# Chunk attention and a Mish feed-forward by seven products: results of a set summed and passed through Mish in place in PSUM, lower parts moved back, weight sums from slot 14, more lower parts on GpSimd

## The chip, the core and the metric

The kernel runs on one core of a Trainium2 chip. Its engines each work through their own instructions in order: TensorE (PE in the profile; PEld is its weight loads), VectorE (DVE), ScalarE (ACT), GpSimd (POOL) and SyncE (SP), which issues nearly all DMAs. An instruction waits on semaphores for what it needs, and everything behind it on its engine waits with it. The metric is the device time in microseconds (us). The kernel before was timed in three runs with a median of 862.57 us, from 860.93 to 862.65.

## What is computed

Attention runs inside chunks of 64 tokens, then a feed-forward layer with the Mish activation follows over 4608 tokens with model width 512 and inner width 2048.

```python
scores = scale * np.matmul(q_c, k_c.transpose(0, 1, 2, 4, 3))     # chunks of 64
attn = softmax(scores)
x = np.matmul(attn, v_c)                                          # (4608, 512) after reordering
h = x @ w_in                                                      # (4608, 2048)
g = h * np.tanh(np.log1p(np.exp(h)))                              # Mish
out = g @ w_out                                                   # (4608, 512)
```

All is float32. The large products are made of three products of rounded parts: each factor is split into a higher part (a cast) and a lower part (the value less its higher part), and high by high, high by low and low by high are added up in PSUM. So each factor costs a cast, called "hi", and a subtraction, called "lo".

## The kernel before, in words

**Two phases.** The first 1024 tokens go through a plain phase of 32 slots, `slot(s)`, s from 0 to 31 (`N` = 32). Slot s runs on TensorE the up projection of step s+1 (`up`), some attention, and the down projection of step s-1 (`down`). Beside it VectorE and ScalarE split the weights (done by slot 14), take Mish, cast (`g_hi`, L327 and L329) and subtract (`g_lo`, L334). The other 3584 tokens go through 32 sets, `s_set(z)`, z from 0 to 31, in four blocks of eight sets: a block is 896 tokens, a set is 256 columns of the inner width.

**A set** makes a 2 by 2 block product with seven products u0 to u6 instead of eight. The order of a set is written out by hand in `ORDER`, fourteen steps m = 0 to 13: the even steps are u0 to u6 (`s_up`, L675, six matmuls of 448 columns each), the odd ones are down projections (`s_down`, L697, six matmuls of 512 columns each) of the set before, d0 to d5, and at step 1 the last one, e6, of the set before that. At each step the program issues the matmuls, then attention that is planned for this step on TensorE, then for a down projection its sum (`s_out`, L724: VectorE adds the PSUM bank to the running sum), and then whatever `when(z, m, ...)` has put there, in the order in which it was put. (z, m) below is step m of set z.

The four results c11, c12, c22 and c21 of a set come out like this. u1 and u0 make c11, u2 and u4 with the copy "u2" make c12, and so on: u0, u3, u5 and u6 add up in one PSUM bank called al (two of them, in turn), u1 goes to a bank b, and u2 and u4 add up in a bank g. ScalarE copies three of these (`s_copy`, L739: "p1" at step 0, "p5" at step 4, "u2" at step 6) to SBUF. VectorE then adds (`s_c`, L748): c11 = b + p1 at step 2, c12 = g + u2 at step 8, c22 = al + p5 at step 10. c21 is al itself after u6. ScalarE takes Mish (`s_hi`, L760) and casts (L761), and VectorE subtracts (`s_lo`, L764): lo 11 at step 3, lo 12 at step 9, lo 22 at step 11, lo 21 at step 13. In the kernel before each c lies in SBUF, in a tile of the tag z.

Waits that tie TensorE to these: u4 adds onto g, so it waits for the copy p5; u5 adds onto al and waits for the copy u2; u6 adds onto al and waits for c22. In set 0 the banks b and g are the two halves of one PSUM tile, bg, and u2 waits for c11.

**The inputs of a block**, seven sums and views of x (`x_sum`, L624; k = 2, 5, 3, 4), are split in the last set of the block before (z = 7, 15, 23): ScalarE casts (`x_hi`, L629), and lo (`x_lo`, L633) runs on GpSimd for k in `LOW_BY_POOL` and on VectorE otherwise. For the first block this is done in slots 29 to 31 and in set 0, all on VectorE but the sum of k = 4. x_sum 4 reads what x_sum 3 wrote, x_hi 4 reads x_sum 4, x_lo 4 reads x_hi 4.

**Weights of the seven products** are made once, in slots 16 to 31: every second slot `t_sum` and `t_diff` (GpSimd, L479 and L493), one slot later `t_hi` (ScalarE, L499), and one slot after that `t_lo` (VectorE, L505) and four DMAs to DRAM (L510). `tset, part = divmod(s - NF, 2)` with NF = 16 says which. They share the four buffers of the tag st with the tiles of `store`, which copies a finished output block out of PSUM at slot 16 and in set 0 (L361 on VectorE, L363 on ScalarE, L367 the DMAs), and with the sum x_sum 2.

**Attention in the sets** (`plan_pair`) starts at the steps `STARTS`; a pair has its maximum on VectorE one and four steps after the start, its subtraction at two and five, Exp on ScalarE (with a table load) at six.

Of the kernel before, what the change touches and what calls it, by code (L numbers as in the profile page):

```python
# [9 lines left out]
F32 = mybir.dt.float32  # L10
# [4 lines left out]
AF = mybir.ActivationFunctionType  # L15
# [3 lines left out]
P = 128  # L19
# [6 lines left out]
def kernel(  # L26
# [437 lines left out]
    def keep_weights(f):  # L464

        s, e = divmod(f, 2)
        for k, half in ((0, 0), (1, 1)) if e == 0 else ((4, 1),):
            src = w_part(f, slice(0, 2))[:, :, half * 2 * P : (half + 1) * 2 * P]
            nc.sync.dma_start(out=raw(dwi_of(s, k)), in_=raw(src))
        nc.sync.dma_start(out=raw(dwo[s][:, e]), in_=raw(w_part(f, slice(2, 4))))  # L470
# [30 lines left out]
    def t_lo(s):  # L501
        d = tw.pop(s)
        for i in range(2):
            o = d["s", i]
            nc.vector.tensor_tensor(  # L505
                out=o[:, :, 1], in0=d["t"][:, 2 * i : 2 * i + 2], in1=raw(o[:, :, 0]), op=ALU.subtract
            )
            for e in range(2):
                k = (2, 3, 5, 6)[2 * i + e]
                nc.sync.dma_start(out=raw(dwi_of(s, k)), in_=raw(o[:, e]))  # L510
# [89 lines left out]
            ps = d["p", t].rearrange("p g c k -> p (g c) k").unsqueeze(1)  # L600
            small_mm(o[:, :, t : t + 1], d["v"][:, t : t + 1], ps, FIRST)

    LOW_BY_POOL = (2, 5, 6)
    xo = {}
    xs = {}

# [24 lines left out]
    def x_lo(b, k):  # L631
        engine = nc.gpsimd if b and k in LOW_BY_POOL else nc.vector
        engine.tensor_tensor(  # L633
            out=xo[k][:, 1], in0=x_src(b, k), in1=raw(xo[k][:, 0]), op=ALU.subtract
        )
# [107 lines left out]
    def s_c(z, n):  # L743

        where, other = C_OF[n]
        o = places["a", z] if where == "a" else places[where]
        ct[z, n] = ew.tile([P, HALF], F32, name=f"c{n}_{z}", tag="z", bufs=2)
        nc.vector.tensor_tensor(out=ct[z, n], in0=o[:, :HALF], in1=ct.pop((z, other)), op=ALU.add)  # L748

    def g_view(z, n, part):  # L750
# [2 lines left out]

    def s_hi(z, n):
        if n == 21:
            src = places["a", z][:, :HALF]
            ct[z, n] = ew.tile([P, HALF], F32, name=f"c{n}_{z}", tag="z", bufs=2)
        else:
            src = ct[z, n]
        nc.scalar.activation(out=ct[z, n], in_=src, func=AF.Mish)  # L760
        nc.scalar.copy(out=g_view(z, n, 0), in_=ct[z, n])  # L761

    def s_lo(z, n):
        nc.vector.tensor_tensor(  # L764
            out=g_view(z, n, 1), in0=ct.pop((z, n)), in1=raw(g_view(z, n, 0)), op=ALU.subtract
        )
# [20 lines left out]
    def slot(s):  # L787
        a = plan.get(s, {})
        e = quick.get(s, {})
        n = 2 * s + 3  # L790
        tset, part = divmod(s - NF, 2)

        if 1 <= s and s + 1 < N:
            up(s + 1, last="w")
        if "norm" in e:
            a_norm(e["norm"])
        if "v" in e:
            a_values(e["v"])
        if "t" in a:
            a_transpose(a["t"])  # L800
        if "v" in a:
            a_values(a["v"])
        if "s" in a:
            a_scores(a["s"])
        if 1 <= s < N - 1:
            down(s - 1)
        if "s" in e:
            a_scores(e["s"])
        if "norm" in e:
            a_transpose(e["norm"])  # L810

        if a.get("load", 0) > PAIRS:
            load_qk(a["load"])
        if "load" in e:
            load_qk(e["load"])
        w("load", n + 4)
        w("hi", n)
        w("scale", n + 2)
        w("bits", n + 1)
        w("lo", n)  # L820
        if "max" in a:
            a_max(a["max"])
        if "max" in e:
            a_max(e["max"])
            a_sub(e["max"])
            load_v(e["max"])
        if "norm" in a:
            if a["norm"] == PAIRS:
                a_inverse(a["norm"])
            a_norm(a["norm"])  # L830
        if "t" in a:
            a_copy(a["t"])
        if "exp" in a:
            a_exp(a["exp"])
        if "max" in e:
            a_exp(e["max"])

        w("load", n + 5)
        if "x" in a:
            a_hi(a["x"])  # L840
        if s < N:
            g_hi(s)
            g_lo(s)
        if s + 1 < N:
            mish(s + 1)
        w("hi", n + 1)
        w("scale", n + 3)
        w("bits", n + 2)
        w("lo", n + 1)
        if "max" in a:  # L850
            a_sub(a["max"])
        if a.get("exp", 0) > PAIRS:
            a_inverse(a["exp"])
        if "max" in e:
            a_inverse(e["max"])
        if "x" in a:
            a_lo(a["x"])
        if "v" in e:
            a_x(e["v"], 0)
            if e["v"] != AHEAD[-1]:  # L860
                a_x(e["v"], 1)
        if "norm" in e:
            a_copy(e["norm"])
        if "max" in a:
            load_v(a["max"])
        if 0 <= s - KEEP < NF:
            keep_weights(s - KEEP)
        if 0 <= tset < NS:
            if part == 0:
                if tset:  # L870
                    t_lo(tset - 1)
                t_sum(tset)
                t_diff(tset)
            else:
                t_hi(tset)
        if s >= 1 and s % NF == 0:
            store(s // NF - 1)
# [3 lines left out]
    def when(z, i, *ops):  # L881
        due.setdefault((z, i), []).extend(ops)
# [4 lines left out]
    def plan_set(z):  # L887

        b, s = divmod(z, NS)
        when(z, 0, lambda: s_copy(z, "p1"))  # L890
        when(z, 1, lambda: wo_load(z))
        when(z, 2, lambda: s_c(z, 11), lambda: s_hi(z, 11))
        when(z, 3, lambda: s_lo(z, 11))
        when(z, 4, lambda: s_copy(z, "p5"))
        when(z, 6, lambda: s_copy(z, "u2"))
        when(z, 8, lambda: s_c(z, 12), lambda: s_hi(z, 12))
        when(z, 9, lambda: s_lo(z, 12))
        when(z, 10, lambda: s_c(z, 22), lambda: s_hi(z, 22))
        when(z, 11, lambda: s_lo(z, 22))
        when(z, 12, lambda: s_hi(z, 21))  # L900
        when(z, 13, lambda: s_lo(z, 21))
        if s == NS - 1 and b + 1 < NSB:
            plan_x(z, b + 1)

    def plan_x(z, b):
        for k in range(7):
            when(z, 2 * k + 1, lambda k=k: x_hi(b, k))
        for k, m in enumerate((1, 3, 5, 6)):
            when(z, m + (k == 3), lambda k=k: x_lo(b, k))
        for k, m in (4, 1), (5, 3), (6, 6):  # L910
            when(z + 1, m, lambda k=k: x_lo(b, k))
        when(z, 0, lambda: x_sum(b, 2))
        when(z, 2, lambda: x_sum(b, 5))
        when(z, 2, lambda: x_sum(b, 3))
        when(z, 4, lambda: x_sum(b, 4))
# [47 lines left out]
    with tc.manual_schedule():  # L963
        prologue()
        for s in range(N - 1):
            slot(s)
            if s == N - 5:
                for g in range(3):
                    ring_load(g)
            if s == N - 3:  # L970
                x_sum(0, 2)
                for m in range(2):
                    x_hi(0, m)
                    x_lo(0, m)
            if s == N - 2:
                a_x(AHEAD[-1], 1)
                x_sum(0, 5)
                x_sum(0, 3)
                x_hi(0, 2)
                x_lo(0, 2)  # L980
                x_hi(0, 3)
                x_sum(0, 4)
        ZN = NSB * NS
        pe[0, 1] = [lambda: down(N - 2, (0, 1))]
        pe[0, 3] = [lambda: down(N - 2, (2, 3))]
        pe[0, 5] = [lambda: down(N - 1, (0, 1))]
        pe[0, 11] = [lambda: down(N - 1, (2, 3))]
        for m, i in (4, 1), (5, 3), (6, 5):
            when(0, i, lambda m=m: x_hi(0, m))
        for m, i in (3, 1), (4, 2), (5, 4), (6, 7):  # L990
            when(0, i, lambda m=m: x_lo(0, m))
        when(0, 3, lambda: t_lo(NS - 1))
        when(0, 5, lambda: store(NB - 1, (0, 1)))
        when(0, 11, lambda: store(NB - 1, (2, 3)))
        slot(N - 1)
        for j, start in zip(range(AHEAD[-1] + 1, NPAIR), STARTS):
            plan_pair(j, start)
        for z in range(ZN):
            plan_set(z)
        s_set(0)  # L1000
        plain.close()
        ps_s = ctx.enter_context(tc.tile_pool(name="ps_s", bufs=1, space=bass.MemoryType.PSUM))
        for n in "b", "g", "d0", "d1":
            places[n] = ps_s.tile([P, DM], F32, name=n, tag=n)
        for z in range(1, ZN + 2):
            s_set(z)
# [38 lines left out]
```

## Time and profile before

| what | value |
|---|---|
| median of three runs | 862.57 us (860.93 to 862.65) |
| the profiled execution's own time | 861.71 us |
| its span, first to last instruction | 859.9 us |
| plain phase, to the first product of set 0 | 220.9 us |
| set 0, from its first product to that of set 1 | 22.4 us |
| sets 26 to 31, from first product to first product | 18.15 us each |
| last instruction of TensorE to the end of the span | about 5 us |

The page lists the busy time of each engine, the chain that ended last, and the costliest groups of instructions. A group's row has its source line, engine, operation, what it writes and reads, its count, its busy time and mean duration, and the idle time of its engine ahead of it with what ended that. A row of the timeline has start and duration in us, engine, line, operation, tiles, shape and count; a bracket at its end holds the idle time before it and what ended it. The end of a matmul is modelled, so pacing is read from starts: six matmuls of 448 columns take 1.21 us from start to the next start and six of 512 take 1.38 us where nothing waits. An undisturbed set is so 7 x (1.21 + 1.38) = 18.15 us.

### The profile page before, as it was taken

How to read it: one execution, taken by the hardware profiler on the slowest of the kernel's cores; microseconds unless marked ns; L12 is line 12 of the kernel's file. 1: busy time of each engine (PE TensorE's matmuls, PEld its weight loads, DVE VectorE, ACT ScalarE, POOL GpSimd, SP SyncE). 2: the span in 40 equal slices, each digit the busy share in tenths (PEclk: the TensorE clock that was granted, in tenths of full speed). 3: DMA queues.
4: the chain of work that ended last, by engine and by line, in shares of the span. 5: the costliest groups of instructions: out<-in, count | busy, mean ns of one | idle time of the engine just before them, and what ended most of it. 6: DMA issues, size and time to landing. Idle time of an engine off the chain costs nothing.

```text
span 859.9 us, 14537 instructions
## 1 busy us (share of the span) xinstructions
PE 835.8 (97%) x5984; PEld 711.0 (83%) x5984; DVE 518.1 (60%) x792; ACT 427.6 (50%) x701; POOL 101.0 (12%) x76
## 2 busy tenths in 40 slices
PE   7989999999799999999999999999999999999997
PEld 7777877888688888888888888888888888888886
DVE  6988884666864647485456557653746563445444
ACT  5987953344465534456635534464435444433331
POOL 0000032544300000240000004200000340000000
PEclk9999999999899999999999999999999999999999
DMA  7656787989584454557656334774445446444513
GB/s 294 223 166 227 221 280 208 340 273 320 196 263 167 165 215 151 206 194 237 228 170 231 142 147 147 244 256 173 167 172 187 145 162 225 162 162 155 187 53 86
DMA packets 51299, 170.82 MB, mean 199 GB/s; under 512 B 5153, under 2 KB 11297, under 8 KB 39969
## 3 DMA queue, kind: packets, MB, share of 16 engines
q1 hardware_dynamic: 50384, 168.45, 56.6%
q10 hardware_dynamic: 848, 1.44, 0.5%
q8 instruction: 47, 0.77, 0.4%
q14 instruction: 20, 0.16, 0.1%
HBM read 137.36 MB, written 32.51 MB: 198 GB/s over the span
## 4 chain that ended last, share of the span: by engine, by line
PE 67%; DVE 3%; ACT 2%; issue 1%; POOL 0%; DVEq 0%
PE d L697 33%; PE al L675 17%; PE g L675 8%; PE b L675 4%; PE av L181 1%; PE s L181 1%; PE pt L583 1%; DVE c L748 1%; DVE g L764 1%; DVE xo L633 1%; ACT c L760 0%; PE bg L675 0%; DVE sum L724 0%; ACT g L761 0%; PE g L697 0%
## 5 line engine op out<-in xcount | busy, mean ns | idle before, releaser
L697 PE MATMUL d<-wo,g 128*128 128x512 f32 x1320 | 338.7, 392 | 0.0
L697 PEld LDWEIGHTS d<-wo,g 128*128 128x128 f32 x1320 | 247.9, 188 | 44.5
L724 DVE TENSOR_TENSOR sum<-d,sum 128x512 f32<-128x512 f32 x192 | 132.4, 690 | 182.2 <-PE d L697 181.8
L675 PE MATMUL al<-xo,ring 128*128 128x448 f32 x768 | 178.4, 368 | 3.0 <-DVE c L748 3.0
L675 PEld LDWEIGHTS al<-xo,ring 128*128 128x128 f32 x768 | 142.5, 188 | 22.0 <-DVE c L748 5.0
L760 ACT ACTIVATE c<-c 128x448 f32<-128x448 f32 x96 | 55.6, 579 | 185.8 <-DVE c L748 185.7
L764 DVE TENSOR_TENSOR g<-c,g 128x448 fp32r<-128x448 f32 x128 | 84.9, 663 | 32.3 <-ACT g L761 32.2
L309 PE MATMUL h<-x,w 128*128 128x512 f32 (+1 forms) x396 | 94.1, 387 | 0.8 <-ACT x L283 0.8
L675 PE MATMUL g<-xo,ring 128*128 128x448 f32 x372 | 86.0, 367 | 1.1 <-ACT p L739 1.1
L309 PEld LDWEIGHTS h<-x,w 128*128 128x128 f32 x396 | 72.4, 189 | 15.6 <-ACT x L283 0.9
L347 PE MATMUL o_o<-w,gh 128*128 128x512 f32 x256 | 80.5, 396 | 0.0
L675 PEld LDWEIGHTS g<-xo,ring 128*128 128x128 f32 x372 | 69.3, 188 | 10.2 <-ACT p L739 2.0
L761 ACT CAST g<-c 128x448 fp32r<-128x448 f32 x128 | 72.6, 567 | 4.1
L347 PEld LDWEIGHTS o_o<-w,gh 128*128 128x128 f32 x256 | 49.0, 191 | 10.1
L347 PE MATMUL o_o<-w,gl 128*128 128x512 f32 x128 | 51.8, 405 | 2.3 <-DVE gl L334 2.3
L624 POOL TENSOR_TENSOR xs<-x 128x896 f32<-128x896 f32 x3 | 6.4, 2122 | 378.5 <-ACT x L524 378.5
L675 PE MATMUL b<-xo,ring 128*128 128x448 f32 x186 | 43.4, 369 | 0.0
L675 PEld LDWEIGHTS b<-xo,ring 128*128 128x128 f32 x186 | 34.3, 188 | 3.7
L479 POOL TENSOR_TENSOR c<-w 128x512 f32<-128x512 f32 x16 | 24.1, 1522 | 111.9 <-DVE w L136 111.9
L739 ACT COPY p<-al 128x448 f32<-128x448 f32 x32 | 17.0, 532 | 36.0 <-PE al L675 35.9
L334 DVE TENSOR_TENSOR gl<-z,gh 128x512 fp32r<-128x512 f32 x32 | 27.5, 858 | 11.2 <-ACT gh L327 10.7
L748 DVE TENSOR_TENSOR c<-b,p 128x448 f32<-128x448 f32 x31 | 19.2, 620 | 24.9 <-PE b L675 24.9
(99 smaller groups left out, 836.2 us busy)
## 6 DMA issues: line engine op xcount, KB each, us to landing
ring<-dwi SPq DMA_DIRECT2D x56, 1024.0 KB, 4.9
wo<-dwo SPq DMA_DIRECT2D x32, 1024.0 KB, 4.9
wis<-in_w_in SPq DMA_DIRECT2D x16, 512.0 KB, 4.5
wos<-in_w_out SPq DMA_DIRECT2D x16, 512.0 KB, 3.9
q<-in_q SPq DMA_DIRECT2D x16, 512.0 KB, 6.4
k<-in_k SPq DMA_DIRECT2D x16, 512.0 KB, 6.6
v<-in_v SPq DMA_DIRECT2D x16, 512.0 KB, 5.7
dwo<-w SPq DMA_DIRECT2D x16, 512.0 KB, 6.8
```

Of the source, the lines that this page charges most:

```text
L181: nc.tensor.matmul(o[h * CHUNK : (h + 1) * CHUNK, c, t - ts.start, g], lhsT=l[rows, t, 2 * g + h], rhs=r[rows, t, 2 * g + h], start=True, ...
L309: nc.tensor.matmul(h[:, cols], lhsT=wi(f, w_, kt), rhs=x[:, kt, cols], start=(n == 0), stop=(n == 3 * NK - 1),)
L334: nc.vector.tensor_tensor(out=d["gl"], in0=d["z"], in1=d["gh"].bitcast(F32), op=ALU.subtract)
L347: nc.tensor.matmul(acc[t], lhsT=g[:, sl], rhs=w_part(f, w_), start=(f == 0 and n == 0), stop=(f == NF - 1 and n == 2),)
L479: nc.gpsimd.tensor_tensor(out=d[e], in0=raw(w_part(f, 0)), in1=raw(w_part(f, 1)), op=ALU.add)
L675: nc.tensor.matmul(o[:, :HALF], lhsT=w_[:, wn, kt * P : (kt + 1) * P], rhs=x[:, xn, kt], start=(n == 0 and k < 3), stop=(n == 5), skip_gro ...
L697: nc.tensor.matmul(o, lhsT=g_tile(z, e)[:, gn, i * P : (i + 1) * P], rhs=wos[z % 2][:, e, wn], start=(n == 0), stop=(n == 5),)
L724: nc.vector.tensor_tensor(out=a, in0=o, in1=a, op=ALU.add)
L748: nc.vector.tensor_tensor(out=ct[z, n], in0=o[:, :HALF], in1=ct.pop((z, other)), op=ALU.add)
L760: nc.scalar.activation(out=ct[z, n], in_=src, func=AF.Mish)
L761: nc.scalar.copy(out=g_view(z, n, 0), in_=ct[z, n])
L764: nc.vector.tensor_tensor(out=g_view(z, n, 1), in0=ct.pop((z, n)), in1=raw(g_view(z, n, 0)), op=ALU.subtract)
```

## The change

From set 1 on, c11 and c12 are written over the PSUM bank that they are summed from, instead of to a tile in SBUF; Mish works in place there, and the cast and the subtraction read that bank. c21 goes through Mish in its bank al in all sets. c22 stays in SBUF, as u6 adds onto its bank.

lo 12 moves from step 9 to 11, lo 22 from 11 to 13, and lo 21 from step 13 to step 1 of the next set.

At block boundaries x_lo 4 goes to GpSimd, and x_lo 4, 5 and 6 move from the next set to steps 9, 11 and 13 of the same set. In set 0, x_lo 4 moves from step 2 to 4 and x_lo 5 from 4 to 5.

The sums for the weights start at slot 14 instead of 16, and the last `t_lo` runs in slot 30 instead of at (0, 3).

```diff
-    LOW_BY_POOL = (2, 5, 6)
+    LOW_BY_POOL = (2, 4, 5, 6)
...
         o = places["a", z] if where == "a" else places[where]
-        ct[z, n] = ew.tile([P, HALF], F32, name=f"c{n}_{z}", tag="z", bufs=2)
+        if z == 0 or n == 22:
+            ct[z, n] = ew.tile([P, HALF], F32, name=f"c{n}_{z}", tag="z", bufs=2)
+        else:
+            ct[z, n] = o[:, :HALF]
...
         if n == 21:
-            src = places["a", z][:, :HALF]
-            ct[z, n] = ew.tile([P, HALF], F32, name=f"c{n}_{z}", tag="z", bufs=2)
-        else:
-            src = ct[z, n]
-        nc.scalar.activation(out=ct[z, n], in_=src, func=AF.Mish)
+            ct[z, n] = places["a", z][:, :HALF]
+        nc.scalar.activation(out=ct[z, n], in_=ct[z, n], func=AF.Mish)
...
-        tset, part = divmod(s - NF, 2)
+        tset, part = divmod(s - NF + 2, 2)
...
+        if part == 0 and 0 < tset <= NS:
+            t_lo(tset - 1)
         if 0 <= tset < NS:
             if part == 0:
-                if tset:
-                    t_lo(tset - 1)
                 t_sum(tset)
...
-        when(z, 9, lambda: s_lo(z, 12))
+        when(z, 11, lambda: s_lo(z, 12))
...
-        when(z, 11, lambda: s_lo(z, 22))
+        when(z, 13, lambda: s_lo(z, 22))
...
-        when(z, 13, lambda: s_lo(z, 21))
+        when(z + 1, 1, lambda: s_lo(z, 21))
...
-        for k, m in enumerate((1, 3, 5, 6)):
-            when(z, m + (k == 3), lambda k=k: x_lo(b, k))
-        for k, m in (4, 1), (5, 3), (6, 6):
-            when(z + 1, m, lambda k=k: x_lo(b, k))
+        for k, m in (0, 1), (1, 3), (3, 7), (2, 5), (4, 9), (5, 11), (6, 13):
+            when(z, m, lambda k=k: x_lo(b, k))
...
-        for m, i in (3, 1), (4, 2), (5, 4), (6, 7):
+        for m, i in (3, 1), (4, 4), (5, 5), (6, 7):
             when(0, i, lambda m=m: x_lo(0, m))
-        when(0, 3, lambda: t_lo(NS - 1))
```

## The prediction

> **What bounds the kernel now.** I read the page's busy times first, then the list of waits, then the timeline around each place where TensorE paused.
>
> ```profile
> span 859.9 us, 14537 instructions
> ...
> PE 835.8 (97%) x5984; PEld 711.0 (83%) x5984; DVE 518.1 (60%) x792; ACT 427.6 (50%) x701; POOL 101.0 (12%) x76
> ...
> PE bg L675 <- DVE c L748: 4.9, 1, 4.9
> ...
> PE al L675 <- DVE c L748: 3.0, 4, 0.8
> ...
> L675 PE MATMUL g<-xo,ring 128*128 128x448 f32 x372 | 86.0, 367 | 1.1 <-ACT p L739 1.1
> ```
>
> TensorE is busy 97% of the span and the change removes none of its matmuls. No other engine is over 60%, so less work elsewhere is worth nothing by itself. What can be won are TensorE's pauses, and in the sets these rows name nearly all of them: one of 4.9 us in set 0 (u2 waits for c11), four of 3.0 us together (u6 waits for c22), and 1.1 us where u4 waits for the copy p5. The rest of the time is matmul pace, the start of the kernel, and its end.
>
> The first pause, engine by engine:
>
> ```profile
> 221.38 1.51 DVE L624 TENSOR_TENSOR x<-xs,x 128x896 f32<-128x896 f32 x1
> 222.82 1.63 DVE L633 TENSOR_TENSOR xo<-xs,xo 128x896 fp32r<-128x896 f32 x1
> 224.37 0.96 DVE L329 CAST gh<-z 128x512 fp32r<-128x512 f32 x1
> 225.36 1.11 DVE L334 TENSOR_TENSOR gl<-z,gh 128x512 fp32r<-128x512 f32 x1
> 226.40 4.11 DVE L633 TENSOR_TENSOR xo<-x,xo 128x896 fp32r<-128x896 f32 x2
> 230.42 0.62 DVE L748 TENSOR_TENSOR c<-bg,p 128x448 f32<-128x448 f32 x1
> ...
> 223.46 1.58 POOL L493 TENSOR_TENSOR t<-c 128x256 f32<-128x256 f32 x1
> 225.89 2.52 POOL L624 TENSOR_TENSOR x<-x 128x896 f32<-128x896 f32 x1
> ...
> 228.44 0.94 ACT L629 CAST xo<-x 128x896 fp32r<-128x896 f32 x1 [1.43 <-POOL x L624]
> ...
> 217.00 1.08 DVE L633 TENSOR_TENSOR xo<-x,xo 128x896 fp32r<-128x896 f32 x1
> ```
>
> c11 ends at 231.04 and u2 starts at 231.18; TensorE has run out of matmuls 4.9 us before, at 226.2 or so. VectorE is packed all the while. Two things make it late. The last row is a lo with GpSimd idle, 1.08; beside GpSimd x_lo 2 takes 1.63 (222.82), and the two of 226.40 take 4.11. Such a row ends when GpSimd's does plus about its own time: VectorE is held while a GpSimd instruction runs. And c11 stands behind x_lo 4, which needs x_hi 4 (228.44), which needs GpSimd's x_sum 4, itself late behind the last t_diff.
>
> The pauses before u6 look like this:
>
> ```profile
> 517.10 2.19 DVE L764 TENSOR_TENSOR g<-c,g 128x448 fp32r<-128x448 f32 x1
> ...
> 533.05 2.14 POOL L633 TENSOR_TENSOR xo<-xs,xo 128x896 fp32r<-128x896 f32 x1
> ...
> 533.76 2.37 DVE L633 TENSOR_TENSOR xo<-x,xo 128x896 fp32r<-128x896 f32 x1
> 536.05 0.61 DVE L748 TENSOR_TENSOR c<-g,u 128x448 f32<-128x448 f32 x1
> 536.59 0.67 DVE L724 TENSOR_TENSOR sum<-d,sum 128x512 f32<-128x512 f32 x1
> 537.91 0.62 DVE L764 TENSOR_TENSOR g<-c,g 128x448 fp32r<-128x448 f32 x1 [0.65 <-ACT g L761]
> 538.45 0.61 DVE L748 TENSOR_TENSOR c<-al,p 128x448 f32<-128x448 f32 x1
> ...
> 534.17 1.54 PE L697 MATMUL d<-wo,g 128*128 128x512 f32 x6
> 535.55 1.38 PE L675 MATMUL al<-xo,ring 128*128 128x448 f32 x6
> 536.76 1.54 PE L697 MATMUL d<-wo,g 128*128 128x512 f32 x6
> 539.12 1.08 PE L675 MATMUL al<-xo,ring 128*128 128x448 f32 x4 [0.82 <-DVE c L748]
> ```
>
> By the starts d takes 1.38 (534.17 to 535.55), so u6 was due at 536.76 + 1.38 = 538.14 and came 0.98 late, where the bracket has 0.82. c22 was late behind lo 12, which sat waiting 0.65 us for ScalarE.
>
> **The change part by part**, against the profiled execution (861.71, 1.8 above its span, 0.86 below the median).
>
> *In place in PSUM.* No instruction comes or goes; 62 adds (c11 and c12 of 31 sets) and 94 Mish (those and 32 c21) write PSUM, and 94 casts and 94 lo read it.
>
> ```profile
> L764 DVE TENSOR_TENSOR g<-c,g x128: 612/617/2477, 232.3 to 844.6; 128x448 fp32r<-128x448 f32 x128
> L748 DVE TENSOR_TENSOR c<-al,p x32: 572/624/626, 240.8 to 840.0; 128x448 f32<-128x448 f32 x32
> ```
>
> The two rows have minimum, median and maximum in ns. An add with one input in PSUM takes 0.624, a lo with both in SBUF 0.617. No row writes PSUM from these engines. I bound it by 0.1 us an instruction either way, and take 0. Nothing of it reaches TensorE: c11 has over 3 us until u4 needs p5 in a quiet set, c12 only feeds the next set. More matters in the third number: lo reaches 2.477, the PSUM adds never over 0.626, though both run beside GpSimd. So I expect a lo from PSUM not to be held. The bank b, g or al is kept until its lo instead of its sum; the next writer is a set later, so no wait there.
>
> [...]
>
> *The moved lo.* lo 12 leaves the way of c22. In the case shown, c22 would start after the sum at 537.2 and end at 537.8, 0.3 ahead of u6. The four pauses go (the lo at 517.10 also runs free): 3.0 us of idle, scaled 0.98/0.82, is 3.6. Taken: -3.6; bounds -3.7 and -1.8 (half of them still late). In exchange lo 22, still with both inputs in SBUF, runs later, and lo 21 comes ahead of c11 of the next set: 0.62 more on VectorE before c11 where an attention pair has its maxima and subtractions there, thus a later Mish, Exp and p5.
>
> ```profile
> 381.19 2.48 DVE L764 TENSOR_TENSOR g<-c,g 128x448 fp32r<-128x448 f32 x1
> 384.79 1.07 DVE L633 TENSOR_TENSOR xo<-x,xo 128x896 fp32r<-128x896 f32 x1
> ...
> 383.60 1.54 PE L697 MATMUL d<-wo,g 128*128 128x512 f32 x6
> ```
>
> Two sets pause for p5 now, 1 and 8, the 1.1 us above. In set 8 the held instruction becomes lo 22, x_lo 4 (1.07) goes and lo 21 (0.62) comes: 0.45 won. In set 1 0.6 is lost. Five other pairs lose 0.6 of their slack too; the list shows no pause there now, so they cost from nothing to 0.6 each. Taken: 0.0 in all; bounds -1.0 and +3.0.
>
> *x_lo on GpSimd.* At three boundaries 2.13 us more of GpSimd and 1.07 less of VectorE. u4 to u6 of the next set need these parts thirteen steps later. Taken 0 beyond the above; bounds -0.3 and +0.5 (a held lo 22 reaching c11).
>
> *Weight sums two slots earlier.* The first t_sum already starts as soon as VectorE has freed its buffers, not when slot 16 comes, so its start stays. t_diff 1 gets a free buffer and need not wait for the output's DMAs, so GpSimd works on beside slots 15 and 16. The first t_lo (two of 0.7) and its four DMAs come before `store` of slot 16, on VectorE and in SP's queue, and its tiles are then reused by `store`.
>
> ```profile
> 136.54 0.69 DVE L361 COPY ob<-o_o 128x512 f32<-128x512 f32 x1 [2.43 <-DMA out<-ob]
> ...
> 137.28 0.50 PE L347 MATMUL o_o<-w,gl 128*128 128x512 f32 x1
> ```
>
> This copy ends at 137.23 and TensorE starts on its bank at 137.28: no slack. Each tenth that the DMAs delay it is lost. VectorE idles long enough here for t_lo, and the DMA queue is empty. Taken +0.3; bounds 0 and +3.
>
> *Set 0.* With the weights done, GpSimd is idle when x_sum 3 ends. From 220.27 on, where x_sum 5 starts, I lay VectorE's work again: x_sum 5 and x_sum 3 at 1.08 each to 222.4, x_lo 2 to 223.5. x_sum 4 then has 2.1 on GpSimd and holds the cast gh (done 0.3 after GpSimd's row at 223.46 now) to 225.9; gl (0.7, the lo's 0.617 for 448 columns brought to 512) to 226.6, x_lo 3 to 227.7, c11 to 228.3, u2 at 228.4 instead of 231.18. The last t_diff is also gone from beside slot 28, so t_lo there, its DMAs and x_sum 2, which waits for them, come up to 1 us earlier; I take half. Taken: -3.3; bounds -1.0 and -5.1 (no pause left). Behind u2, x_lo 4 is back at about 231, u4 due at 234: no new wait.
>
> *The clock.* After the pause the granted clock was halved, and also after a shorter one (in the rows of a stretch the second number is TensorE's busy time, the third from the end the clock granted):
>
> ```profile
> 52.66 0.50 PE L347 MATMUL o_o<-w,gl 128*128 128x512 f32 x1 [2.33 <-DVE gl L334]
> ...
> 50.70:54.10 3.40, 1.44 (x6) 1.22 (x7) 3.33 (x6) 0.76 (x3) 0.00 (x0) 1.00 0.22 88
> 54.10:57.50 3.40, 3.40 (x9) 2.65 (x9) 3.37 (x6) 3.40 (x7) 0.00 (x0) 0.50 0.59 164
> 224.80:228.20 3.40, 1.43 (x7) 0.83 (x5) 3.37 (x3) 1.05 (x2) 3.40 (x3) 1.00 1.04 342
> 231.60:235.00 3.40, 3.40 (x10) 2.85 (x10) 2.35 (x4) 2.65 (x5) 0.00 (x0) 0.50 0.76 258
> ```
>
> From 231.18 to 235.0 at half speed cost half of 3.8, 1.9 us. Both times the clock fell behind a stretch of 3.4 us in which TensorE ran 1.4. A pause of 1.8 or so leaves it at least 1.6 in any such stretch, mostly over 2. Taken: the clock holds, -1.9; bounds -1.9 and 0.
>
> [...]
>
> *Sum:* -3.6 + 0.0 + 0 + 0.3 - 3.3 - 1.9 = -8.5. 861.71 - 8.5 = 853.2 in the profiled execution's time, and 862.57 - 8.5 = 854.1 against the median. I say 854.5.
>
> **The rivals.**
> 1. *The entry stays slow:* c11 comes near 229 or the clock falls again, and the new p5 waits eat part of the u6 gain. For it: x_lo 3 and x_lo 2 still have two SBUF inputs. Then about -1.5 at the entry, -2.5 in the sets: 858.5.
> 2. *The store of slot 16 is late:* its copies wait for the landing of t_lo's DMAs, TensorE idles some 3 us, the clock falls for 1.7. With the rest of the forecast 854.5 + 4.5 = 859.0; with rival 1, 863, which is no change.
> 3. *Slower: d0 waits for the moved lo 21.* lo 21 now runs behind the sum of e6, and d0 reads the same tile of g. If the wait is for the whole tile, it decides from the moment that lo 21 ends after d0's weights load.
>
> ```profile
> 828.46 0.69 DVE L724 TENSOR_TENSOR sum<-d,sum 128x512 f32<-128x512 f32 x1 [1.37 <-PE d L697]
> 829.47 1.54 PE L697 MATMUL d<-wo,g 128*128 128x512 f32 x6
> ```
>
> lo 21 would run from 829.07 to 829.69, so d0 would start at about 830.0 instead of 829.47: 0.5 us in 31 sets, 15 us, and 854.5 + 15 = 869.5. Against it: at 383.60 d0 starts while lo 21 of its set (381.19 for 2.48) still runs, so it waits only for the columns that it reads.
>
> **How the numbers follow.** Forecast 0.62, between 851 and 858; rival 1 0.20; rival 2 0.11; rival 3 0.07. Two runs of this kernel can be told apart by about 0.2%, 1.7 us: faster means under 860.8. Faster: 0.62 + 0.17 + 0.06 = 0.85; same 0.03 + 0.05 = 0.08; slower 0.07. The range goes from 850.5 (the lower bounds of set 0, p5, the slots and x_lo, 3.4 in all, and the 0.6 that runs scatter by) to 861, past rivals 1 and 2 alone; it leaves out rival 3 and the sum of 1 and 2.
>
> **What would show it.** u2 of set 0 within 2.5 us of the matmul before it, at full clock after; no lo from PSUM over 0.7; no u6 waiting for c22 in the list of waits; p5's row about as long as before; no pause at slot 17. A d0 that waits for a subtraction, or a half clock after set 0's pause, makes it wrong.

## The result and the profile after

The changed kernel took 851.84 us, the median of four runs (851.0 to 852.21), where the kernel before took 861.86 beside it (860.93 to 862.65). The ratio is 0.988, its 95% interval 0.987 to 0.990. The forecast was 854.5, its range 850.5 to 861.0.

First the page of the changed kernel: the span, the busy time of the engines, and the groups to set beside those of before.

```profile
span 849.1 us, 14607 instructions
...
PE 832.2 (98%) x5984; PEld 709.1 (84%) x5984; DVE 510.5 (60%) x789; ACT 420.2 (49%) x701; POOL 105.2 (12%) x79
...
L675 PE MATMUL g<-xo,ring 128*128 128x448 f32 x372 | 85.9, 366 | 0.3 <-ACT p L739 0.3
L760 ACT ACTIVATE b<-b 128x448 f32<-128x448 f32 x31 | 16.4, 528 | 73.5 <-DVE b L751 73.5
```

TensorE has the same 5984 matmuls and shorter pauses. Those are named in the list of waits of the changed kernel (total, times, longest):

```profile
PE o_o L347 <- DVE gl L334: 2.4, 1, 2.4
PE bg L675 <- DVE c L751: 1.7, 1, 1.7
PE s L181 <- PE o_o L347: 0.9, 1, 0.9
PE g L675 <- ACT p L739: 0.3, 1, 0.3
```

The row of u6 waiting for c22 (3.0, four times) is gone, u2's wait in set 0 went from 4.9 to 1.7, u4's wait for p5 from 1.1 to 0.3. No row has d0 waiting for a subtraction. Then the timeline of the changed kernel at the entry of set 0:

```profile
222.27 1.09 DVE L633 TENSOR_TENSOR xo<-xs,xo 128x896 fp32r<-128x896 f32 x1
223.27 2.36 DVE L329 CAST gh<-z 128x512 fp32r<-128x512 f32 x1
225.67 0.69 DVE L334 TENSOR_TENSOR gl<-z,gh 128x512 fp32r<-128x512 f32 x1
226.28 1.08 DVE L633 TENSOR_TENSOR xo<-x,xo 128x896 fp32r<-128x896 f32 x1
227.28 0.62 DVE L751 TENSOR_TENSOR c<-bg,p 128x448 f32<-128x448 f32 x1
...
222.52 2.83 POOL L624 TENSOR_TENSOR x<-x 128x896 f32<-128x896 f32 x1 [15.49 <-DVE x L624]
...
227.95 1.50 PE L675 MATMUL bg<-xo,ring 128*128 128x448 f32 x6 [1.72 <-DVE c L751]
...
224.80:228.20 3.40, 1.68 (x8) 1.08 (x7) 3.06 (x4) 1.21 (x2) 0.55 (x1) 1.00 0.93 333
231.60:235.00 3.40, 3.40 (x18) 3.04 (x17) 2.84 (x5) 1.54 (x4) 0.00 (x0) 1.00 0.59 132
```

GpSimd has only x_sum 4 left here, the cast gh is held once (2.36), c11 ends at 227.90, and the granted clock (in the last two rows, which are stretches, the third number from the end) stays at 1.00 behind the pause.

**Where the time went.** I lined up the two traces by the start of TensorE's first product of each set. What was won between two such starts belongs to the set between them:

| part | forecast | measured |
|---|---|---|
| slots, up to the first product of set 0 | +0.3 | 0.0 |
| set 0, with the clock | -5.2 | -4.96 |
| p5 waits, sets 1 and 8 | 0.0 | -0.58 and -0.44 |
| u6 waits, sets 13, 14, 15, 23 | -3.6 | -3.73 |
| all other sets | 0.0 | -0.35 |
| behind TensorE's last matmul | 0.0 | -0.73 |
| sum | -8.5 | -10.79 |

The 0.0 of the first row is not the price of the edits there. By the first matmul of the down projection, the changed trace was 0.66 us ahead in slot 1 (33.19 against 33.85), where nothing was edited, still 0.42 ahead in slot 17 (135.19 against 135.61), and 0.04 behind in slot 19 (149.05 against 149.01). So it lost 0.46 between slots 17 and 19, beside the store of slot 16. The seven other traces with the early weight sums lose 0.23 to 1.28 there, the three with the late ones gain 0.14 to 0.23. The start of set 0's first product lies anywhere from 219.7 to 223.8 in these traces, so that the two starts agree is chance.

The row before the sum is landing time of the last output. VectorE's last sum ends 4.3 us ahead of the end of the span before (859.9) and 3.6 ahead of it after (849.1):

```profile
854.90 0.69 DVE L724 TENSOR_TENSOR sum<-g,sum 128x512 f32<-128x512 f32 x1 [0.67 <-PE g L697]
```

```profile
844.85 0.69 DVE L724 TENSOR_TENSOR sum<-g,sum 128x512 f32<-128x512 f32 x1 [0.67 <-PE g L697]
```

No edit touches it. In the experiments' profiled executions it was again 0.7 shorter than before in all but one, also in the kernel before with one part alone (PSUM alone, below). So it is rather the one trace of the kernel before that ended late.

### The profile page after: what moved, and what is told of

Same layout as the page of the kernel before. It is cut to its first block, busy times and chain, and to the rows that moved or that the text cites. A ratio compares the mean times of both kernels' runs of the same rounds, so it can differ in the third digit from the quotient of the medians.

```text
span 849.1 us, 14607 instructions
## 1 busy us (share of the span) xinstructions
PE 832.2 (98%) x5984; PEld 709.1 (84%) x5984; DVE 510.5 (60%) x789; ACT 420.2 (49%) x701; POOL 105.2 (12%) x79
## 3 DMA queue, kind: packets, MB, share of 16 engines
q10 hardware_dynamic: 848, 1.44, 0.5%
## 4 chain that ended last, share of the span: by engine, by line
PE 88%; DVE 6%; ACT 3%; DMA 2%; issue 1%; SPq 0%; POOL 0%; DVEq 0%; ACTq 0%; POOLq 0%
PE d L697 35%; PE al L675 18%; PE g L675 9%; PE o_o L347 8%; PE h L309 7%; PE b L675 4%; PE s L181 2%; PE av L181 2%; PE pt L583 1%; PE pt L252 1%; DMA k<-in_k 1%; DMA dwi<-ts 1%; DVE r L236 1%; DVE m L208 1%; PE spare L377 0%
## 5 line engine op out<-in xcount | busy, mean ns | idle before, releaser
L760 ACT ACTIVATE b<-b 128x448 f32<-128x448 f32 x31 | 16.4, 528 | 73.5 <-DVE b L751 73.5
L760 ACT ACTIVATE g<-g 128x448 f32<-128x448 f32 x31 | 16.4, 528 | 70.8 <-DVE g L751 70.8
L760 ACT ACTIVATE c<-c 128x448 f32<-128x448 f32 x34 | 19.6, 578 | 37.6 <-DVE c L751 37.6
L347 PEld LDWEIGHTS o_o<-w,gl 128*128 128x128 f32 x128 | 24.4, 191 | 8.5 <-DVE gl L334 2.8
```

Of the source, the lines that this page charges most:

```text
L347: nc.tensor.matmul(acc[t], lhsT=g[:, sl], rhs=w_part(f, w_), start=(f == 0 and n == 0), stop=(f == NF - 1 and n == 2),)
L760: nc.scalar.activation(out=ct[z, n], in_=ct[z, n], func=AF.Mish)
```

## The experiments

Each is the changed kernel with one part undone (the first five) or the kernel before with one part alone (the next two); the last three build on the changed kernel. Times are compared through the kernel before, run beside each, since its median moved from 861.0 to 863.2 from one group of runs to another. For each, the columns behind the ratio say what its profiled execution won over that of before, in us, by set:

| kernel | median us | ratio to before (95%) | set 0 | set 1 | set 8 | 13 to 15 | 23 |
|---|---|---|---|---|---|---|---|
| changed | 851.84 | 0.988 (0.987 to 0.990) | 4.96 | 0.58 | 0.44 | 2.86 | 0.87 |
| weight sums late | 855.40 | 0.992 (0.989 to 0.995) | 1.95 | 0.58 | 0.45 | 2.81 | 0.81 |
| x_lo 4 early | 854.93 | 0.991 (0.988 to 0.993) | 2.38 | 0.58 | 0.54 | 2.80 | 0.87 |
| results in SBUF | 852.58 | 0.988 (0.985 to 0.990) | 4.81 | 0.58 | 1.08 | 2.73 | 0.73 |
| lower parts early | 854.75 | 0.991 (0.988 to 0.994) | 5.26 | 0.08 | 1.07 | 1.44 | 0.18 |
| x_lo 4 on VectorE | 852.16 | 0.989 (0.987 to 0.991) | 4.91 | 0.58 | -0.28 | 2.86 | 0.86 |
| PSUM alone | 857.76 | 0.995 (0.993 to 0.996) | 0.98 | 0.08 | 1.04 | 1.45 | 0.19 |
| moved lower parts alone | 859.02 | 0.996 (0.994 to 0.998) | -0.42 | 0.58 | -0.62 | 2.70 | 0.68 |
| x_sum 4 on VectorE | 850.74 | 0.987 (0.985 to 0.988) | 7.03 | 0.39 | 0.52 | 2.80 | 0.81 |
| early in set 7 too | 848.93 | 0.986 (0.984 to 0.988) | 7.04 | 0.47 | 1.07 | 2.88 | 0.84 |
| changed, again | 850.44 | 0.988 (0.986 to 0.990) | 5.11 | 0.58 | 0.45 | 2.83 | 0.85 |

From set 1 on the sets repeat within 0.2 us where nothing was edited; the times scatter by more. Set 0, with its pause and the clock behind it, differs by 1 us between two traces with no edit ahead of the pause (PSUM alone, point 3). So the verdicts below rest on the sets, and on set 0 only where it moves by more than that.

**1. Set 0: the weight sums or the order of x_lo 4?** Weight sums back at slot 16:

```diff
-        tset, part = divmod(s - NF + 2, 2)
+        tset, part = divmod(s - NF, 2)
...
+        when(0, 3, lambda: t_lo(NS - 1))
```

> The changed kernel with the weight sums back at slot 16 (last t_lo at (0, 3)); all else as changed. The changed kernel took 851.84 us. Theory (it is the weight sums' early end that makes room in set 0: with them late, x_sum 4 stands behind the last t_diff on GpSimd again): x_sum 4 ends near 228.4 instead of 225.3, c11 of set 0 ends near 230, TensorE's pause before u2 goes from 1.9 us back to about 3.9, the granted clock falls behind it (1.9 us): about 855.5, and the u6 waits stay away. Rival (the order of x_lo 4 and 5 in set 0 gives the gain): about 1 us, 853, pause of u2 under 3 us.

Set 0's own part of the order back:

```diff
-        for m, i in (3, 1), (4, 4), (5, 5), (6, 7):
+        for m, i in (3, 1), (4, 2), (5, 4), (6, 7):
```

> The changed kernel with set 0's x_lo 4 and 5 back at steps 2 and 4, ahead of c11; all else as changed. Theory: c11 is later by x_lo 4 (1.08 us, VectorE, GpSimd idle by then), the pause before u2 goes from 1.9 to about 2.9 us and the clock may or may not fall behind it: 852.9 if it holds, 854.8 if it falls. Rival (this order is the main cause of set 0's gain): the pause is back near 4.9 and the clock falls, about 856.5.

The timeline of the first, TensorE, VectorE and GpSimd, and a stretch behind u2's start:

```profile
228.27 1.08 PE L675 MATMUL bg<-xo,ring 128*128 128x448 f32 x4 [3.20 <-DVE c L751]
...
224.72 2.96 DVE L633 TENSOR_TENSOR xo<-x,xo 128x896 fp32r<-128x896 f32 x1
...
223.33 0.92 POOL L493 TENSOR_TENSOR t<-c,t 128x256 f32<-128x256 f32 x1
224.21 2.52 POOL L624 TENSOR_TENSOR x<-x 128x896 f32<-128x896 f32 x1
...
228.30:231.70 3.40, 3.40 (x12) 2.83 (x13) 3.35 (x5) 3.20 (x5) 0.00 (x0) 0.70 0.66 224
```

x_sum 4 stands behind the last t_diff again, and it is now x_lo 3, right ahead of c11, that is held (2.96). In the second it is x_lo 4 that delays c11, with GpSimd idle:

```profile
231.99 1.25 PE L675 MATMUL bg<-xo,ring 128*128 128x448 f32 x5 [2.84 <-DVE c L751]
...
232.00:235.40 3.40, 3.40 (x12) 2.83 (x13) 1.72 (x2) 3.13 (x5) 0.00 (x0) 0.69 0.24 101
```

Set 0 lost 3.0 us in the first and 2.6 in the second, of the 4.96 that the whole change wins there. In both about half is the longer wait (1.5 and 1.1 by the brackets) and the rest the clock, which fell each time. So neither edit alone is the cause: with both the clock held, with either alone it fell, and each alone gets less than half. The theory held for the first (the pause came to 3.2 us for its 3.9), and for the second in its branch where the clock falls.

**2. The u6 waits: where lo 12 stands, or where it reads?** Results in SBUF, with the moved lower parts:

```diff
-        if z == 0 or n == 22:
-            ct[z, n] = ew.tile([P, HALF], F32, name=f"c{n}_{z}", tag="z", bufs=2)
-        else:
-            ct[z, n] = o[:, :HALF]
+        ct[z, n] = ew.tile([P, HALF], F32, name=f"c{n}_{z}", tag="z", bufs=2)
```

(c21 also goes to such a tile in `s_hi`.)

> The changed kernel with all results in SBUF tiles as before the change (c21 through the tile too); the moved lower parts, the weight sums and the rest as changed. Theory (u6's waits went because lo 12 no longer stands ahead of c22, wherever lo reads from): no u6 wait, at most 0.8 us from slower lo 12 or 21 held by GpSimd or from 94 Mish on SBUF: 851.8 to 852.6. Rival (the lo from PSUM is not held by GpSimd and that is what removes the waits): the four u6 waits are back, 3.6 us, about 855.4.

The other way round, results in PSUM with the lower parts at their old steps:

```diff
-        when(z, 11, lambda: s_lo(z, 12))
+        when(z, 9, lambda: s_lo(z, 12))
...
-        when(z, 13, lambda: s_lo(z, 22))
+        when(z, 11, lambda: s_lo(z, 22))
...
-        when(z + 1, 1, lambda: s_lo(z, 21))
+        when(z, 13, lambda: s_lo(z, 21))
```

> The changed kernel with lo 12, lo 22 and lo 21 back at steps 9, 11 and 13; the results stay in PSUM. Theory (position of lo 12): u6 waits for c22 again in sets 13, 15 and 23 (some 0.9 us each), not in 14 where the held lo was one that now reads PSUM, and u4 of set 1 waits for p5 again (0.6): about 855. Rival (reading from PSUM removes the hold and with it the waits): no wait back, 851.8.

In the first the list has no u6 wait. In the second it has three, as expected, and set 1's wait for p5 is back too:

```profile
PE al L675 <- DVE c L751: 1.7, 3, 0.6
...
PE g L675 <- ACT p L739: 0.2, 1, 0.2
```

The theory held: the move takes the waits away, PSUM alone removes one (set 14) and shortens the others.

**3. The same two parts, each alone on the kernel before.** (The edits are those of the diff above. Its guard around `t_lo` came along in both; with the sums still starting at slot 16 it runs the same `t_lo` in the same slots.)

> The kernel before with the results in PSUM alone: lower parts, weight sums, x_lo and set 0 as before the change. The kernel before took 861.86 us. Theory (in place in PSUM only shortens a lo that GpSimd would hold): the u6 wait of set 14 goes, those of 13, 15 and 23 stay, set 0's 4.9 us pause stays: about 860.9. Rival (all u6 waits go by it): about 858.2.

> The kernel before with the moved lower parts alone (lo 12 at step 11, lo 22 at 13, lo 21 at step 1 of the next set); results in SBUF, set 0 and the rest as before the change. Theory: the four u6 waits go (3.6 us) and set 1's p5 wait too (0.6), as c22 of set 0 and with it the copies behind it come earlier: about 857.6; x_lo 4 still ahead of c11 in set 8, where lo 21 now stands too, may give back up to 0.6. Rival (set 1's wait went by something else, and held lo 12 or 22 delays other things): about 860.

PSUM alone came out faster than its theory, near the rival's number but not by its mechanism: the list still holds three u6 waits of 1.7 us. The theory had left out set 8. There lo 21 was held for 2.48 us before the change; from PSUM it is not held, and u4's wait goes (1.04). That, set 14 (1.12) and the shorter u6 waits make 2.9 from set 1 on. The 0.98 of set 0 is not the edit's, as nothing ahead of the pause differs: the first of GpSimd's last t_diff rows began 0.8 earlier against u0 in this execution, and the pause was 4.20 instead of 4.95.

The moved lower parts alone won 3.6 us from set 1 to 23, with set 1's wait gone and the four u6 waits gone, but set 8 lost 0.62, where lo 21 and x_lo 4 now both stand ahead of c11. Its twelve runs go from 855.09 to 862.31, so the median settles no half microsecond. Either part alone wins the 1.12 of set 14, which is the main reason why they do not add up.

**4. Where x_lo 4 is made.**

```diff
-    LOW_BY_POOL = (2, 4, 5, 6)
+    LOW_BY_POOL = (2, 5, 6)
...
-        for k, m in (0, 1), (1, 3), (3, 7), (2, 5), (4, 9), (5, 11), (6, 13):
-            when(z, m, lambda k=k: x_lo(b, k))
+        for k, m in enumerate((1, 3, 5, 6)):
+            when(z, m + (k == 3), lambda k=k: x_lo(b, k))
+        for k, m in (4, 1), (5, 3), (6, 6):
+            when(z + 1, m, lambda k=k: x_lo(b, k))
```

> The changed kernel with x_lo 4 on VectorE and x_lo 4, 5, 6 back in the next set (steps 1, 3, 6); all else as changed. Theory (x_lo 4 ahead of c11 of sets 8, 16 and 24 delays that set's p5): u4 of set 8 waits some 1.0 us longer than its 0.44 now, sets 16 and 24 have slack: 852.5 to 853. Rival (u4's wait in set 8 comes from the held lo 22 alone, the place of x_lo 4 costs nothing): 851.8.

```profile
PE g L675 <- ACT p L739: 1.1, 1, 1.1
```

Set 8's wait for p5 is 1.1 instead of 0.3, and set 8 is 0.72 longer; sets 16 and 24 lost nothing. The theory's mechanism holds, at less than its price; in the median it does not show.

**5. What is left in set 0.** x_sum 4, the only thing that GpSimd still did there, moved to VectorE, behind c11:

```diff
-        engine = nc.gpsimd if b or k == 4 else nc.vector
+        engine = nc.gpsimd if b else nc.vector
...
-                x_sum(0, 4)
...
-        for m, i in (4, 1), (5, 3), (6, 5):
+        when(0, 3, lambda: x_sum(0, 4))
+        for m, i in (4, 3), (5, 3), (6, 5):
...
-        for m, i in (3, 1), (4, 4), (5, 5), (6, 7):
+        for m, i in (3, 3), (4, 4), (5, 5), (6, 7):
```

> The changed kernel with set 0's x_sum 4 on VectorE at step 3, behind c11 (instead of on GpSimd in slot 30), and x_hi 4 and x_lo 3 moved to step 3 behind it. Theory (what still delays u2 in set 0 is VectorE held by x_sum 4 on GpSimd, 1.9 us, and x_lo 3 ahead of c11): c11 ends near 225.6, u2's pause of 1.9 us goes: about 850.0. Rival (another wait takes its place: u3 or u4 for the parts of x that are now late): the pause moves to u3 or u4, 851.8 or more.

```profile
222.28 0.42 DVE L329 CAST gh<-z 128x512 fp32r<-128x512 f32 x1
222.73 0.69 DVE L334 TENSOR_TENSOR gl<-z,gh 128x512 fp32r<-128x512 f32 x1
224.17 0.62 DVE L751 TENSOR_TENSOR c<-bg,p 128x448 f32<-128x448 f32 x1 [0.75 <-PE bg L675]
...
225.28 1.38 PE L675 MATMUL bg<-xo,ring 128*128 128x448 f32 x6
```

The same cast takes 0.42 instead of 2.36, VectorE now waits for TensorE ahead of c11, and u2 follows with no pause. Set 0 won 2.07 more than in the changed kernel, and set 1 gave back 0.19. The theory held.

**6. Set 8's last wait.** In the results-in-SBUF kernel set 8 had no wait at all, though its lo 22 stands at the same step. The timelines of the changed kernel and of that one, GpSimd's x_lo and VectorE's lo 22:

```profile
371.36 6.29 POOL L633 TENSOR_TENSOR xo<-x,xo 128x896 fp32r<-128x896 f32 x3 [3.53 <-ACT xo L629]
...
375.66 2.48 DVE L764 TENSOR_TENSOR g<-c,g 128x448 fp32r<-128x448 f32 x1
```

```profile
377.46 0.71 DVE L764 TENSOR_TENSOR g<-c,g 128x448 fp32r<-128x448 f32 x1
...
377.65 2.51 POOL L633 TENSOR_TENSOR xo<-x,xo 128x896 fp32r<-128x896 f32 x1
```

In the changed kernel lo 22 starts 0.13 us behind GpSimd's third x_lo (which starts at 375.53) and is held to its end. In the other it starts 0.2 ahead of it, runs in 0.71, and it is GpSimd that takes 2.51 instead of 2.12. Two tenths decide between 0.7 and 2.5. So lo 22 of set 7, and with it the other two, went back to the early steps, in that set alone and on top of the version of point 5:

```diff
-        when(z, 11, lambda: s_lo(z, 12))
+        when(z, 9 if z == 7 else 11, lambda: s_lo(z, 12))
...
-        when(z, 13, lambda: s_lo(z, 22))
+        when(z, 11 if z == 7 else 13, lambda: s_lo(z, 22))
...
-        when(z + 1, 1, lambda: s_lo(z, 21))
+        when(*((z, 13) if z == 7 else (z + 1, 1)), lambda: s_lo(z, 21))
```

> The version with set 0's x_sum 4 on VectorE (850.7 us), and in set 7 alone the three lower parts back at steps 9, 11 and 13. Theory (u4 of set 8 waits 0.44 us because lo 22 at step 13 starts just behind GpSimd's third x_lo and is held for 2.5 us; at step 11 it misses it): set 8 gains 0.4 to 0.6, its lo 22 under 1.2 us, no u6 wait in set 7; about 850.2, which the times hardly show and the trace does. Rival (the lower parts of set 7 meet another GpSimd row or c22 is late): set 8's wait stays, or u6 of set 7 waits: 850.7 or more.

> The changed kernel once more, unaltered, on the chip of the run above, for a comparison there and for what one kernel's profiled executions scatter by: some 851.8. Theory on the scatter (first product of set 0 from 219.7 to 223.8 us and sets of 18.15 or 18.34 us after set 24 belong to the execution, not to the kernel): either may differ here from the first profile, set 0 and the sets' waits repeat within 0.2 us. Rival (they belong to the kernel's code): all of it repeats.

```profile
371.29 1.09 DVE L764 TENSOR_TENSOR g<-c,g 128x448 fp32r<-128x448 f32 x1 [0.65 <-ACT g L761]
```

lo 22 takes 1.09, no matmul of a set waits for another engine in its list any more, and set 8 won 1.07 instead of 0.44; set 7 lost 0.13. At 848.93 against 850.44 for the changed kernel on the same chip, this version has the lowest median here. The two intervals overlap, so the times alone would not separate them; the 1.9 of set 0 and the 0.5 of sets 7 and 8, trace against trace, do.

## Why the prediction was right, point by point

**u6 waits: right**, -3.73 for -3.6, and by the step it named: lo 12 out of c22's way (experiment 2).

**In place in PSUM: right where it was used, and more than the step allowed.** The bound of 0.1 us an instruction held: Mish takes 0.528 in place, against 0.579 in SBUF. That a lo from PSUM is not held is shown by the lower parts of the changed kernel, shapes apart (the three numbers are minimum, median and maximum in ns):

```profile
L764 DVE TENSOR_TENSOR g<-c,g x34: 615/617/2476, 229.1 to 834.6; 128x448 fp32r<-128x448 f32 x34
L764 DVE TENSOR_TENSOR g<-al,g x32: 608/615/624, 240.5 to 835.9; 128x448 fp32r<-128x448 f32 x32
L764 DVE TENSOR_TENSOR g<-b,g x31: 614/616/626, 243.5 to 821.6; 128x448 fp32r<-128x448 f32 x31
L764 DVE TENSOR_TENSOR g<-g,g x31: 614/615/620, 252.4 to 832.0; 128x448 fp32r<-128x448 f32 x31
```

Eight of the 94 rows of the last three lines ran beside a GpSimd instruction, and none took over 0.626. The medians are level: 0.617 with the value in SBUF, 0.615 and 0.616 with it in PSUM.

"Nothing of it reaches TensorE" is true of the changed kernel, where the results in SBUF win as much in the sets, and false of this part alone, which is worth 2.9 us (experiment 3).

**p5: the step that failed.** Forecast 0.0 as -0.45 for set 8 and +0.6 for set 1. Set 8 came as said: -0.44, with lo 22 as the held instruction. Set 1 won 0.58 instead of losing 0.6. The step counted lo 21 as 0.62 us more ahead of c11 and took the start of that row of work as fixed. It is not. Before, then after, VectorE at the end of set 0:

```profile
240.25 0.63 DVE L764 TENSOR_TENSOR g<-c,g 128x448 fp32r<-128x448 f32 x1 [1.25 <-ACT g L761]
240.79 0.62 DVE L748 TENSOR_TENSOR c<-al,p 128x448 f32<-128x448 f32 x1
243.13 0.69 DVE L361 COPY ob<-o_o 128x512 f32<-128x512 f32 x1 [1.73 <-ACT ob L363]
...
247.46 0.61 DVE L748 TENSOR_TENSOR c<-b,p 128x448 f32<-128x448 f32 x1
```

```profile
234.59 0.62 DVE L751 TENSOR_TENSOR c<-al,p 128x448 f32<-128x448 f32 x1 [0.56 <-PE al L675]
236.94 0.69 DVE L361 COPY ob<-o_o 128x512 f32<-128x512 f32 x1 [1.73 <-ACT ob L363]
...
241.67 0.62 DVE L751 TENSOR_TENSOR b<-b,p 128x448 f32<-128x448 f32 x1
```

lo 12 stood ahead of c22 with 1.25 us of waiting for its cast. Without it c22 starts as soon as TensorE is done, and Mish, cast and the copies of the output behind it follow 1.2 us earlier. The copy ob is 0.1 ahead of the first product of set 1 (243.24) before, 1.3 ahead of it (238.28) after. From that copy to c11 it takes 0.4 more after, as one lo more stands there (4.33, then 4.73). That leaves c11 0.8 earlier against set 1's first product: 4.22 behind it, then 3.39. All versions with lo 12 moved win 0.4 to 0.6 in set 1, the two without it 0.08.

**x_lo on GpSimd: right at 0** in itself, and its place is worth 0.7 in set 8 (experiment 4), which the forecast had inside its -0.45.

**Weight sums and the store: right in size (+0.3, and 0.46 lost between slots 17 and 19), by a small margin.** Rival 2's wait did come, without its 3 us: the copy of slot 16 waits for the landing of t_lo's DMAs.

```profile
134.07 0.69 DVE L361 COPY ob<-o_o 128x512 f32<-128x512 f32 x1 [3.27 <-DMA dwi<-ts]
136.22 0.69 DVE L361 COPY ob<-o_o 128x512 f32<-128x512 f32 x1 [1.45 <-ACT ob L363]
...
136.97 0.49 PE L347 MATMUL o_o<-w,gl 128*128 128x512 f32 x1
```

It ends almost early enough: the second copy ends at 136.91 and its matmul starts 0.3 late, where it was 0.2 late before. The rest of the 0.46 is lost in the two slots behind it, for a cause that is not shown. In two of the other seven traces with the early sums TensorE waits longer here, as in that of the lower parts early:

```profile
137.12 0.50 PE L347 MATMUL o_o<-w,gl 128*128 128x512 f32 x1 [0.82 <-DVE ob L361]
```

**Set 0: right**, -4.96 for -5.2, u2 at 227.95 for 228.4. One step in it did not come: x_sum 2 was to start up to 1 us earlier, half of it taken, and started 0.13 earlier (214.86 for 214.99). VectorE's rows, which overlap by about 0.1 each, made up for it. **The clock held**, as forecast, and the pause was short enough for that wherever it fell (below). **Rivals 1 and 3** did not come: the entry is fast, and no matmul d waits for a lo.

So of the 2.3 us by which the trace beat the sum (-8.5 against -10.79), 1.2 is set 1's sign and 0.7 the landing of the last output, which scatters; the rest are small terms of both signs. The forecast of 854.5 had besides been rounded up by 0.4 from 854.1.

## What to carry to other kernels

When an instruction leaves the way of a waiting one, follow the second one's successors too: what starts earlier can outweigh what the first one costs at its new place, as in set 1. Where the clock falls behind a long pause, the last microsecond taken off it is worth more than itself: undoing either of two edits made set 0's pause 1.1 to 1.5 us longer and cost 2.6 to 3.0. On an engine that another one can hold, ask which of the two starts first: here a few tenths of a microsecond decided (0.13 behind GpSimd's start lo 22 took 2.48 us, 0.2 ahead of it 0.71), and moving an input to PSUM (0.626 at most), or the other engine's work away (the cast at 0.42 instead of 2.36), settled it.

## What the runs showed of the hardware

**The one that started second was held.** Experiment 6 has both orders: lo 22 on VectorE took 2.48 us behind GpSimd's start and 0.71 ahead of it, and in the second case x_lo on GpSimd took 2.51 instead of 2.12. In the changed kernel a lo with both inputs in SBUF took 2.476 at most, one that reads PSUM 0.626. A cast with a single SBUF input was held as well (2.36 beside x_sum 4, and 0.42 with GpSimd idle).

**The clock does not fall by the length of the pause alone.** The changed kernel twice, with the same pause at the fourth down projection; its first matmul and two stretches (TensorE's busy time is the second number, the granted clock the third from the end):

```profile
52.04 0.50 PE L347 MATMUL o_o<-w,gl 128*128 128x512 f32 x1 [2.36 <-DVE gl L334]
...
49.23:52.64 3.41, 1.05 (x5) 0.54 (x5) 3.27 (x7) 1.48 (x3) 0.00 (x0) 1.00 0.35 139
52.64:56.05 3.41, 3.41 (x10) 2.63 (x9) 3.38 (x6) 2.71 (x5) 0.00 (x0) 0.50 0.39 136
```

```profile
53.16 0.50 PE L347 MATMUL o_o<-w,gl 128*128 128x512 f32 x1 [2.37 <-DVE gl L334]
...
51.39:54.81 3.42, 1.65 (x7) 1.40 (x8) 3.38 (x5) 0.78 (x2) 0.00 (x0) 1.00 0.19 78
54.81:58.22 3.41, 3.41 (x16) 2.83 (x16) 3.34 (x7) 3.41 (x7) 0.00 (x0) 1.00 0.63 168
```

Over the twelve traces, the 2.33 to 2.56 us there halved the clock in eight and not in four. In set 0 five pauses of 2.8 us or more all did, and five of 1.4 to 2.0 did not, one of them (1.98) with TensorE busy 1.43 of a 3.4 us stretch, by which the prediction would have had it fall.

The traces say what decides. Within each trace the granted clock changes only at times that are whole multiples of 3.413 us apart (before the change 14, 1, 50, 2 and 183 of them in turn), so each execution has a fixed row of stretches, and the four above are such stretches. Of all 2954 of them at full clock (247 before the change, 246 in the changed kernel's first trace), the clock was halved behind each of the 26 (three and two in these traces) in which TensorE was busy 1.46 us or less, and behind none of the others, which have 1.62 or more. The pause of 1.98 had 1.62 in its stretch. So a pause of some 1.7 us, as in the changed kernel's set 0 (1.68 left in the worst 3.4 us), could lie anywhere; one of 2.4 falls into one stretch or is shared by two, by chance; and the falls behind 2.84 and 3.20 us in experiment 1 were likely but not certain.

The stretch at half speed cost 1.6 us: from that matmul to the start of the up projection behind it 4.44 us passed in the changed kernel (52.04 to 56.48), and 2.85 in the results-in-SBUF kernel (55.28 to 58.13), where the clock held. As one kernel had both outcomes, this alone can scatter its times by as much.

**Left open.** In three of the profiled executions (weight sums late, moved lower parts alone, x_sum 4 on VectorE) the sets from 24 on took 18.34 us instead of 18.15 at a full granted clock, 1.5 us up to TensorE's last matmul. No run here shows why, nor whether it belongs to the kernel or to the execution.
